# Attention with routing logits: logits from a queue with a rate per group, keys made in two parts, score goes kept whole

## The chip, the core and the metric

The program runs on one core of a Trainium2 chip. The time is the device time of one execution in microseconds, taken as the median of several runs. TensorE multiplies matrices into PSUM, VectorE and ScalarE read and write PSUM and SBUF, GpSimd and SyncE mainly issue transfers here. In the profile the engines are named PE, PEld (TensorE's weight loads), DVE (VectorE), ACT (ScalarE), POOL (GpSimd) and SP (SyncE).

## What is computed

Eight batches of 2496 rows go through an attention with squared ReLU scores; every row of the result is then sent to one of 8 experts, in the order of the logits, each expert taking at most 2496 rows.

```
scores = z @ z.T / 2496                  # per batch, 2496 x 2496, z has 64 columns
x = u * (maximum(scores, 0)**2 @ v)      # 2496 x 256 per batch
logits = x @ w_gate                      # 19968 x 8
order = argsort(-logits.flatten())       # greedy: a row goes to the first expert with room
out[rows of e] = maximum(x[rows of e] @ w1[e], 0) @ w2[e]
```

## The kernel before

The first part, `attention`, takes some 1440 us of the 2565 us span, and the change touches only it. The rows of a batch form 20 key tiles of 128 (the last one of 64 rows, `NT` = 19, `KT` = 20) and five groups of query columns (`NQ` = 5): groups 0 to 3 of 512 columns, group 4 of 448. `seq` lists all 8 x 5 x 20 steps (batch, group, key tile).

For each key tile the scores of a group are three matmuls (`sc`, line 802), since every f32 number is split into a high and a low part. The contraction has 64 rows, so two tiles are multiplied side by side. Ten tiles are done together, in a *go* (`scores`, 30 matmuls): their results leave PSUM through ReLU and scale into `a`, four tiles by VectorE (line 806) and six by ScalarE (line 808). A go is written four steps ahead of the first tile that it serves, so the first go of a group stands before the last four tiles of the group ahead of it. ScalarE then squares each `a` (line 816) and copies it to `hi` (line 820), and VectorE makes `lo` = a - hi (line 829; for the 64-row tile it writes into the same buffer, line 826). `av` multiplies hi and lo with the split values `vh`, `vl` and adds them up in two PSUM tiles, `acc0` and `acc1` (lines 852 to 855; in group 4 with the operands exchanged, lines 844 to 847). There is one buffer of each. At the end of a group VectorE multiplies them with `u` into `xs` (line 865) or, in group 4, `xt` (line 874), and the next group's first matmul into `acc0` may start only when that has read `acc0`. In this document that place is called a *turn*: the turn of group 2 is the passage from group 2 to group 3, and the batch turn that from group 4 to the next batch's group 0.

The logits of a finished group are 32 VectorE instructions (`post_logits`, line 908, tile `lt`): 4 blocks of 128 rows for 8 experts, each a product with a row of weights, added up along the row. They are spread over the steps of the next group. When all logits of a batch are there, `settle` picks each row's best expert and makes sortable keys from its logit (lines 73 to 91 and 104 to 105), at the start of group 2 of the next batch. During each group some z tiles (`zl`, line 772), and in group 4 the 20 value tiles of the next batch (`vl`, line 779), are split on VectorE as well.

All this is written into a table by step, `todo`, and walked in the order of steps. A list scheduler then sets the order of each engine's instructions by readiness in its own model of time; a pin, as in `scores`, keeps squares and splits behind the copies of a go. On the chip every engine then runs its instructions in that fixed order.

Of the kernel before, what the change touches and what calls it, by code (L numbers as in the profile page):

```python
# [21 lines left out]
def tile_attention_then_moe(ctx, tc, u, ut, v, z, w_gate, w1, w2, out):  # L22
# [40 lines left out]
    nc.vector.tensor_scalar(first["at0"], at0_f, 4096.0, -32768.0, op0=OP.mult, op1=OP.add)  # L63

    attention(tc, u, ut, v, z, w_gate, xd, identf, made, first, 1.0 / S)
    moe(tc, xd, first, jp, identf, w1, w2, out, B, S, consts)


def best_expert(nc, pool, first, c, eq):
    lg, m, code, oh = [first[n][:, c] for n in ("lg", "m", "code", "oh")]  # L70
    shape = list(lg.shape)
    cb = first["code8b"][:, None, :].to_broadcast(shape)
    nc.vector.tensor_reduce(m, lg, axis=AX.X, op=OP.max)
    nc.vector.tensor_tensor(eq, lg, m[:, :, None].to_broadcast(shape), op=OP.is_ge)
    nc.vector.tensor_mul(eq, eq, cb)
    nc.vector.tensor_max(eq[:, :, :4], eq[:, :, :4], eq[:, :, 4:])
    nc.vector.tensor_max(eq[:, :, :2], eq[:, :, :2], eq[:, :, 2:4])
    nc.vector.tensor_max(code, eq[:, :, 0], eq[:, :, 1])
    nc.vector.tensor_tensor(oh, code[:, :, None].to_broadcast(shape), cb, op=OP.is_equal)


def order_keys(nc, first, c):
    m, sign, key, rep, top, low = [first[n][:, c] for n in ("m", "sign", "key", "rep", "top", "low")]
    m = m.bitcast(I32)
    nc.vector.tensor_scalar(sign, m, 31, 0x7FFFFFFF, op0=OP.arith_shift_right, op1=OP.bitwise_and)
    nc.vector.scalar_tensor_tensor(key, m, 0x8000, sign, op0=OP.bitwise_xor, op1=OP.bitwise_xor)
    half = key.bitcast(I16).rearrange("p (j h) -> p j h", h=2)
    n = half.shape[1]
    spread(nc, rep, half[:, :, 1])
    nc.vector.tensor_scalar(top, half[:, :, 1], 65536.0, None, op0=OP.mult)  # L90
    nc.vector.tensor_copy(low, half[:, :, 0])
# [9 lines left out]
def spread(nc, rep, x):  # L101
    n = x.shape[1]
    h = n // 2
    nc.scalar.activation(rep[:, :h], x[:, :h, None].to_broadcast([128, h, 8]), AF.Copy)
    nc.vector.tensor_copy(rep[:, h:], x[:, h:, None].to_broadcast([128, n - h, 8]))
# [586 lines left out]
def attention(tc, u, ut, v, z, w_gate, xd, identf, made, first, scale):  # L692
    nc = tc.nc
# [3 lines left out]
    E = lg.shape[2]  # L697
    NT = S // 128
    TL = S - NT * 128
    KT = NT + 1  # L700
    DH = D // 128
    NQ = KT // 4
# [5 lines left out]
    with ExitStack() as ctx:  # L708
# [39 lines left out]
        def load_z(b, g):  # L748
            t = io.tile([128, 512], F32, name="zin")
            for c in range(2):  # L750
                nc.sync.dma_start(t[c * DQ:(c + 1) * DQ], z[b, :, g * 512:(g + 1) * 512])
            ZI[b, g] = t
# [31 lines left out]
        def width(g):  # L784
            return min(512, S - 512 * g)
# [4 lines left out]
        def scores(n, tiles):  # L790
            end = n + tiles
            for n in range(n, end, 2):
                b, g, kt = seq[n]
                w = width(g)
                q = slice(g * 512, g * 512 + w)
                zh, zl = ZH[b], ZL[b]
                p = [ps.tile([128, 512], F32, name="sc", bufs=6)[:, :w] for _ in range(2)]
                for i, (x, y) in enumerate(((zh, zh), (zh, zl), (zl, zh))):
                    for c in range(2):
                        r = slice(c * DQ, (c + 1) * DQ)  # L800
                        k = slice((kt + c) * 128, (kt + c + 1) * 128)
                        nc.tensor.matmul(p[c], x[r, k], y[r, q], start=(i == 0), stop=(i == 2))  # L802
                for c in range(2):
                    a = wk.tile([128, 512], F32, name="a", bufs=GO + 2)[:, :w]
                    if c and n + 2 < end:
                        i = nc.vector.tensor_scalar(a, p[c], 0.0, scale, op0=OP.max, op1=OP.mult)  # L806
                    else:
                        i = nc.scalar.activation(a, p[c], AF.Relu, scale=scale)  # L808
                    A[n + c] = a
                    last[i.ins.engine] = i.ins  # L810
            go.close()
            for i in last.values():
                go.enter_context(tc.issue_after(i))
# [106 lines left out]
            r = slice(TL, 128) if b % 2 else slice(0, TL)  # L920
            nc.vector.tensor_copy(lg[r, B * NT + b // 2], p[r, n * E:(n + 1) * E])

        def settle(lo, hi):
            if lo == hi:
                return
            eq = wk.tile([128, max(NT, B), E], BF, name="eq", bufs=1)
            best_expert(nc, wk, first, slice(lo, hi), eq[:, :hi - lo])
            order_keys(nc, first, slice(lo, hi))

        def premask(lo, hi):  # L930
            at_least(nc, first["mask0"], first["rep"], first["at0"], lo, hi)

        todo = {}
        N = len(seq)

        def at(n, f, *a):
            todo.setdefault(n, []).append((f, a))
# [1 line left out]
        for c in range(0, (B - 1) * NT // 16 * 16, 16):  # L939
            at((B * NQ - 1) * KT + 2 + c // 16, premask, c, c + 16)  # L940
        for b in range(B - 1):
            at(((b + 1) * NQ + 2) * KT, settle, b * NT, (b + 1) * NT)
        at(B * NQ * KT, settle, (B - 1) * NT, (B - 1) * NT + 4 * (NQ - 1))
        at(B * NQ * KT, premask, (B - 1) * NT // 16 * 16, JP - 16)
        for b in range(B):
            for g in range(NQ):
                n0 = (b * NQ + g) * KT
                m0 = n0 + KT
                for d in range(2):
                    at(m0 - 1 if d == 0 else m0 - .5, post_mul if g < NQ - 1 else tail_mul, b, *((g, d) if g < NQ - 1 else (d,)))  # L950
                    if g == NQ - 1:
                        at(m0 + 1 + d if m0 < N else N + 2, tail_turn, b, d)
                t0 = 1 if g < NQ - 1 else 2
                for t in range(4 * E if m0 < N else 0):
                    at(m0 + t0 + t * (KT - 1 - t0) // (4 * E), post_logits, b, g, t // E, t % E)
                if b or g:
                    at(n0 - 3, load_u, b, g)
            n0 = b * NQ * KT
            if b == B - 1:
                at(N + 1, last_logits, b, NQ - 1)  # L960
                at(B * NQ * KT + 3, settle, b * NT + 4 * (NQ - 1), (b + 1) * NT)
                at(B * NQ * KT + 3, settle, B * NT, J)
            if b:
                for g in range(NQ):
                    m = n0 - 3 * KT + 4 * g
                    at(m - 4, load_z, b, g)
                    at(m, z_split, b, g)
                    at(n0 - KT + 4 * g - 8, load_v, b, g)
                for kt in range(KT):
                    at(n0 - KT + kt, split_v, b, kt)  # L970
            else:
                for kt in range(KT):
                    at(kt - 4, split_v, 0, kt)
                for g in range(1, NQ):
                    at((-LA, -2, 2, 4)[g - 1], z_split, 0, g)
                    if g >= 3:
                        at(2 * g - 7, load_z, 0, g)
                        at(4 * g - 11, load_v, 0, g)

        load_z(0, 0)  # L980
        load_v(0, 0)
# [10 lines left out]
        for n in range(-LA, N + 4 * E):  # L992
            if n == 2:
                early.close()
            for k in sorted(k for k in todo if k < n):
                for f, a in todo.pop(k):
                    f(*a)
            if n + LA in goes:
                scores(n + LA, goes[n + LA])
            if 0 <= n + 4 < N:  # L1000
                square(n + 4)
            if 0 <= n + 3 < N:
                split_lo(n + 3)
            if 0 <= n + 4 < N:
                split_hi(n + 4)
            if 0 <= n < N and n % 2 == 0:
                av(n)
            for f, a in todo.pop(n, []):
                f(*a)
# [36 lines left out]
```

## Time and profile before

| | |
|---|---|
| median of 3 runs | 2567.59 us (2567.3 to 2568.21) |
| profiled execution | 2566.36 us, its span 2564.6 us |
| PE busy in the span | 2476.9 us (97%), 19465 matmuls |
| DVE busy | 2035.4 us (79%), 6057 instructions |
| ACT busy | 1526.3 us (60%), 2882 instructions |
| chain that ended last, by engine | PE 85%, DVE 10%, ACT 2% |

Busy time of an engine is the union of its instructions' times; for PE the ends are modelled. The chain that ended last follows the work back from the last instruction to whatever released each step. A row of the timeline gives start and duration in us, engine, line, operation, tiles and shapes, how many equal instructions in a row it stands for, and, in brackets, the idle time ahead of it with what ended it. Instructions of one engine overlap a little in their recorded times, so the step from one start to the next tells how long one holds the engine.

### The profile page before, as it was taken

Reading aid. Unit: us, or ns where it says so; the run is one execution under the profiler, and the core shown is the slowest. Engines: PE = TensorE matmul, PEld = TensorE weight load, DVE = VectorE, ACT = ScalarE, POOL = GpSimd, SP = SyncE. Lnnn points to the kernel's source line nnn. Section 1 sums busy time; section 2 is a strip of 40 time slices with the busy share of each in tenths; the row PEclk is TensorE's granted clock in tenths of the full one; section 3 lists DMA queues with packets and bytes.
Section 4 is the critical chain, followed back from the end, with each engine's and each line's share of the span. In section 5 each row is a group of like instructions: output and inputs, shape, how many; then the busy total and the mean of one; then the engine's idle time right before and its main releaser. Section 6 shows DMA issues by size and latency. Waiting matters only on the chain.

```text
span 2564.6 us, 51297 instructions
## 1 busy us (share of the span) xinstructions
PE 2476.9 (97%) x19465; PEld 2269.6 (88%) x19465; DVE 2035.4 (79%) x6057; ACT 1526.3 (60%) x2882; POOL 359.7 (14%) x507
## 2 busy tenths in 40 slices
PE   8999999999999999999999669999999999999998
PEld 7989989989999999899899557898988898989997
DVE  7898898898898989989988777969695959595322
ACT  8888888797887888878887312333232323233332
POOL 2000000000000000000000003333333333234331
PEclk9999999999999999999999869999999999999999
DMA  5111120121111111111110011211121212131110
GB/s 157 45 59 42 54 74 21 50 74 41 48 58 48 55 58 54 50 41 41 49 33 10 16 42 49 75 49 66 40 72 41 70 42 71 40 99 50 49 40 24
DMA packets 49191, 134.39 MB, mean 52 GB/s; under 512 B 9520, under 2 KB 13104, under 8 KB 48944
## 3 DMA queue, kind: packets, MB, share of 16 engines
q1 hardware_dynamic: 33840, 90.20, 10.9%
q0 software_dynamic: 15104, 40.91, 5.0%
q8 instruction: 152, 2.49, 0.4%
q14 instruction: 95, 0.78, 0.1%
HBM read 90.19 MB, written 40.89 MB: 51 GB/s over the span
## 4 chain that ended last, share of the span: by engine, by line
PE 85%; DVE 10%; ACT 2%; issue 1%; DMA 1%; POOL 0%; POOLq 0%; SPq 0%; ACTq 0%; DVEq 0%
PE acc L852 11%; PE acc L855 11%; PE acc L854 10%; PE sc L802 10%; PE hp L557 5%; PE y L588 5%; PE y L590 5%; PE y L589 5%; PE hp L558 5%; PE hp L559 5%; PE acc L844 2%; PE acc L847 2%; PE acc L846 2%; PE srch L241 2%; DVE lt L908 1%
## 5 line engine op out<-in xcount | busy, mean ns | idle before, releaser
L852 PE MATMUL acc<-vh,hi 128*128 128x256 f32 x2560 | 727.8, 287 | 8.6 <-DVE xs L865 4.7
L855 PE MATMUL acc<-vl,hi 128*128 128x256 f32 x2560 | 718.3, 283 | 0.0
L854 PE MATMUL acc<-vh,lo 128*128 128x256 f32 x2432 | 688.6, 283 | 0.0
L852 PEld LDWEIGHTS acc<-vh,hi 128*128 128x128 f32 x2560 | 489.8, 192 | 37.2 <-issue 22.6
L576 ACT ACTIVATE hh<-hp 128x512 fp32r<-128x512 f32 (+1 forms) x320 | 187.6, 587 | 550.0 <-PE hp L559 460.2
L829 DVE TENSOR_TENSOR lo<-a,hi 128x512 fp32r<-128x512 f32 (+1 forms) x760 | 501.1, 674 | 14.8 <-ACT hi L820 12.6
L855 PEld LDWEIGHTS acc<-vl,hi 128*128 128x128 f32 x2560 | 490.6, 192 | 0.0
L820 ACT ACTIVATE hi<-a 128x512 fp32r<-128x512 f32 (+1 forms) x800 | 470.5, 615 | 29.6 <-ACT a L816 18.9
L908 DVE SCALAR_TENSOR_TENSOR lt<-xs,wgb 128x256 bf16<-128x256 f32 x1248 | 469.5, 421 | 1.6
L854 PEld LDWEIGHTS acc<-vh,lo 128*128 128x128 f32 x2432 | 466.2, 192 | 0.7 <-issue 0.7
L816 ACT ACTIVATE a<-a 128x512 f32<-128x512 f32 (+1 forms) x800 | 463.0, 614 | 0.0
L808 ACT ACTIVATE a<-sc 128x512 f32<-128x512 f32 (+1 forms) x481 | 273.6, 587 | 217.0 <-PE sc L802 191.8
L588 PE MATMUL y<-w2h,hh 128*128 128x256 f32 (+1 forms) x1280 | 365.6, 286 | 0.0
L589 PE MATMUL y<-w2l,hh 128*128 128x256 f32 (+1 forms) x1280 | 361.9, 283 | 0.0
L806 DVE TENSOR_SCALAR a<-sc 128x512 f32<-128x512 f32 (+1 forms) x319 | 210.6, 677 | 138.1 <-PE sc L802 138.0
L557 PE MATMUL hp<-xh,w1h 128*128 128x512 f32 (+2 forms) x646 | 262.6, 408 | 0.7 <-ACT xh L550 0.7
L558 PE MATMUL hp<-xl,w1h 128*128 128x512 f32 (+2 forms) x646 | 251.0, 389 | 0.0
L559 PE MATMUL hp<-xh,w1l 128*128 128x512 f32 (+2 forms) x646 | 249.9, 387 | 0.0
L588 PEld LDWEIGHTS y<-w2h,hh 128*128 128x128 f32 (+1 forms) x1280 | 240.4, 188 | 10.2
L589 PEld LDWEIGHTS y<-w2l,hh 128*128 128x128 f32 (+1 forms) x1280 | 240.2, 188 | 9.0
L621 POOL DMA_INDIRECT out_dram<-y,idx x160 | 179.5, 1122 | 383.7 <-ACT y L615 335.8
L482 POOL DMA_INDIRECT xg<-xd,idx x160 | 161.6, 1010 | 386.7 <-PE xp L541 134.5
(1150 smaller groups left out, 4057.5 us busy)
## 6 DMA issues: line engine op xcount, KB each, us to landing
vr<-in_v_dram SPq DMA_DIRECT2D x32, 512.0 KB, 3.6
ur<-in_u_dram SPq DMA_DIRECT2D x32, 512.0 KB, 4.2
xd<-xs SPq DMA_DIRECT2D x32, 512.0 KB, 2.9
wr<-in_moe_w_dram SPq DMA_DIRECT2D x32, 512.0 KB, 5.0
zin<-in_z_dram SPq DMA_DIRECT2D x80, 128.0 KB, 2.7
ut<-in_ut_dram SPq DMA_DIRECT2D x8, 448.0 KB, 3.8
vr<-in_v_dram SPq DMA_DIRECT2D x8, 384.0 KB, 3.3
xd<-xs SPq DMA_DIRECT2D x8, 384.0 KB, 2.3
```

Source lines behind the costliest of these rows:

```text
L557: nc.tensor.matmul(p[:, c], wh, xh, start=(d == 0), stop=False)
L558: nc.tensor.matmul(p[:, c], wh, xl, start=False, stop=False)
L559: nc.tensor.matmul(p[:, c], wl, xh, start=False, stop=(d == DH - 1))
L588: nc.tensor.matmul(o, h[:, c], wh, start=first, stop=False, skip_group_check=True)
L589: nc.tensor.matmul(o, h[:, c], wl, start=False, stop=False, skip_group_check=True)
L816: nc.scalar.activation(A[n], A[n], AF.Square)
L820: nc.scalar.activation(h, A[n], AF.Copy)
L829: nc.vector.tensor_sub(l, a, h.bitcast(F32))
L852: nc.tensor.matmul(o, h[:, c], vh, start=first and a == 0, stop=False, skip_group_check=True)
L854: nc.tensor.matmul(o, l[:, c], vh, start=False, stop=False, skip_group_check=True)
L855: nc.tensor.matmul(o, h[:, c], vl, start=False, stop=last, skip_group_check=True)
L908: nc.vector.scalar_tensor_tensor(t[r], XS[b, g][r, i], 1.0, WG["rows"][r, e], op0=OP.mult, op1=OP.mult, accum_out=lg[r, j, e:e + 1])
```

## The change

1. A batch's logits go through one queue. A group's 32 logits enter it one step after the group ends (three after group 4), and a step in group g takes RATE[g]/20 of them out: 37, 31, 38, 38 and 18 per group instead of 32. In the last group of the last batch the rate is that of group 0.
2. `settle` for batches 0 to 6 is cut in two, `choose` (best expert) and `rank_keys`, and moved from the start of group 2 of the next batch to steps 12 and 14 of its group 1.
3. The first matmul of the last pair of a go is pinned behind the matmul written before it.

```
-                        nc.tensor.matmul(p[c], x[r, k], y[r, q], start=(i == 0), stop=(i == 2))
+                        mm = nc.tensor.matmul(p[c], x[r, k], y[r, q], start=(i == 0), stop=(i == 2))
+                        if n + tiles == end and i == c == 0:
+                            tc.keep_in_program_order(mm)
...
-        def settle(lo, hi):
-            if lo == hi:
-                return
+        def choose(lo, hi):
             eq = wk.tile([128, max(NT, B), E], BF, name="eq", bufs=1)
             best_expert(nc, wk, first, slice(lo, hi), eq[:, :hi - lo])
+
+        def rank_keys(lo, hi):
             order_keys(nc, first, slice(lo, hi))
+
+        def settle(lo, hi):
+            if lo < hi:
+                choose(lo, hi)
+                rank_keys(lo, hi)
...
         for b in range(B - 1):
-            at(((b + 1) * NQ + 2) * KT, settle, b * NT, (b + 1) * NT)
+            for i, part in enumerate((choose, rank_keys)):
+                at(((b + 1) * NQ + 1) * KT + 12 + 2 * i, part, b * NT, (b + 1) * NT)
...
-                t0 = 1 if g < NQ - 1 else 2
-                for t in range(4 * E if m0 < N else 0):
-                    at(m0 + t0 + t * (KT - 1 - t0) // (4 * E), post_logits, b, g, t // E, t % E)
+                if m0 < N:
+                    ready[m0 + 1 if g < NQ - 1 else m0 + 3] = b, g
...
+        RATE = (37, 31, 38, 38, 18)
+        assert NQ == len(RATE)
+        queue, credit = [], 0.0
+        for n in range(N):
+            if n in ready:
+                queue += [(*ready[n], i, e) for i in range(4) for e in range(E)]
+            g = n // KT % NQ
+            credit += RATE[g if n < N - KT else 0] / KT
+            while queue and credit >= 1:
+                credit -= 1
+                at(n, post_logits, *queue.pop(0))
+            credit = min(credit, 1)
+        assert not queue
```

What this does to the engines' order is shown at three places. In the new file a line of `attention` after the first edit has a number two higher (a logit is L910, `xs` L867).

VectorE in batch 1 at the turn of group 0, from the four copies of the go to the second product; before:

```order
L806 TENSOR_SCALAR a<-sc 128x512 x4
L826 TENSOR_TENSOR hi<-a,hi 64x512
L908 SCALAR_TENSOR_TENSOR lt,lg<-xs,wgb 64x256 x5
L829 TENSOR_TENSOR lo<-a,hi 128x512 x2
L865 TENSOR_TENSOR xs<-acc_2894,ur 128x512
L829 TENSOR_TENSOR lo<-a,hi 128x512
L865 TENSOR_TENSOR xs<-acc_2895,ur 128x512
```

The same place on VectorE now:

```order
L808 TENSOR_SCALAR a<-sc 128x512 x4
L828 TENSOR_TENSOR hi<-a,hi 64x512
L910 SCALAR_TENSOR_TENSOR lt,lg<-xs,wgb 128x256 x8
L831 TENSOR_TENSOR lo<-a,hi 128x512 x2
L910 SCALAR_TENSOR_TENSOR lt,lg<-xs,wgb 128x256
L910 SCALAR_TENSOR_TENSOR lt,lg<-xs,wgb 64x256
L867 TENSOR_TENSOR xs<-acc_2866,ur 128x512
L831 TENSOR_TENSOR lo<-a,hi 128x512
L867 TENSOR_TENSOR xs<-acc_2867,ur 128x512
```

Ten logits stand ahead of the first product where five stood. At the turn of group 1 the order now is the same (8 logits, 2 lo, 2 logits, product); there, before, 5 logits, 11 instructions of `settle` and 2 lo stood ahead of it.

VectorE at the batch turn from batch 0 to 1, from the copies of the go to the first `xt`; before:

```order
L806 TENSOR_SCALAR a<-sc 128x512 x4
L826 TENSOR_TENSOR hi<-a,hi 64x448
L908 SCALAR_TENSOR_TENSOR lt,lg<-xs,wgb 128x256 x5
L779 TENSOR_TENSOR vl<-vr,vh 128x256
L829 TENSOR_TENSOR lo<-a,hi 128x512
L779 TENSOR_TENSOR vl<-vr,vh 128x256
L874 TENSOR_TENSOR xt<-acc_2398,ut 128x448
```

The same place on VectorE now:

```order
L808 TENSOR_SCALAR a<-sc 128x512 x4
L828 TENSOR_TENSOR hi<-a,hi 64x448
L910 SCALAR_TENSOR_TENSOR lt,lg<-xs,wgb 128x256 x6
L779 TENSOR_TENSOR vl<-vr,vh 128x256
L910 SCALAR_TENSOR_TENSOR lt,lg<-xs,wgb 128x256
L831 TENSOR_TENSOR lo<-a,hi 128x512
L779 TENSOR_TENSOR vl<-vr,vh 128x256
L910 SCALAR_TENSOR_TENSOR lt,lg<-xs,wgb 128x256
L831 TENSOR_TENSOR lo<-a,hi 128x512
L876 TENSOR_TENSOR xt<-acc_2398,ut 128x448
```

Three more logits and one more lo stand ahead of `xt`. In the second half of group 4, ahead of these copies, 9 logits now stand where 18 stood.

TensorE in batch 1 at the turn of group 2, from the last matmuls of the old group to the first of the new one (`acc_4532`, now `acc_4524`); before:

```order
L852 MATMUL acc_3968<-vh,hi 128x256
L855 MATMUL acc_3968<-vl,hi 128x256
L802 MATMUL sc<-zh 128x512 x2
L802 MATMUL sc<-zl,zh 128x512 x2
L852 MATMUL acc_4532<-vh,hi 128x256
L854 MATMUL acc_4532<-vh,lo 128x256
```

The same place on TensorE now:

```order
L854 MATMUL acc_3962<-vh,hi 128x256
L857 MATMUL acc_3962<-vl,hi 128x256
L854 MATMUL acc_4524<-vh,hi 128x256
L856 MATMUL acc_4524<-vh,lo 128x256
L857 MATMUL acc_4524<-vl,hi 128x256
```

The four score matmuls that stood in the turn are back in their go, which has 30 again instead of 26. There VectorE has 7 logits, a zl, a lo, 2 logits and 2 lo ahead of the product, where it had 5 logits, a zl and 3 lo. In the same way the one score matmul in each turn of group 3 is gone.

## Rows read from the trace of the kernel before

**Rows 1.** Busy time of each engine in the first 1440 us.

```profile
core 0: us, PE busy (x) PEld busy (x) DVE busy (x) ACT busy (x) POOL busy (x), PEclk, DMA share, GB/s
0.00:1440.00 1440.00, 1419.91 (x10949) 1314.07 (x10950) 1273.28 (x4038) 1183.22 (x2308) 17.05 (x186) 1.00 0.16 52
```

**Rows 2.** Waits of PE until 1420 us: us in total, times, longest.

```profile
PE sc L802 <- DVE a L806: 5.5, 7, 0.8
...
PE acc L852 <- DVE xs L865: 4.7, 7, 0.7
```

**Rows 3.** Timeline of DVE, batch 1, turn of group 1.

```profile
258.75 2.74 DVE L806 TENSOR_SCALAR a<-sc 128x512 f32<-128x512 f32 x4 [3.11 <-PE sc L802]
...
262.24 0.42 DVE L908 SCALAR_TENSOR_TENSOR lt<-xs,wgb 128x256 bf16<-128x256 f32 x1
...
263.98 0.30 DVE L73 TENSOR_REDUCE m<-lg 128x19 f32<-128x152 f32 x1
...
266.71 0.68 DVE L865 TENSOR_TENSOR xs<-acc,ur 128x512 f32<-128x512 f32 x1
```

**Rows 4.** Timeline of PE, same turn: the go's first matmul, the new group's first.

```profile
257.72 0.50 PE L802 MATMUL sc<-zh 64*128 64x512 f32 x2
...
267.54 0.36 PE L852 MATMUL acc<-vh,hi 128*128 128x256 f32 x1 [0.67 <-DVE xs L865]
```

**Rows 5.** Timeline of DVE, batch 1, turn of group 0.

```profile
222.83 2.74 DVE L806 TENSOR_SCALAR a<-sc 128x512 f32<-128x512 f32 x4 [2.89 <-PE sc L802]
...
226.32 0.42 DVE L908 SCALAR_TENSOR_TENSOR lt<-xs,wgb 64x256 bf16<-64x256 f32 x1
...
229.79 0.69 DVE L865 TENSOR_TENSOR xs<-acc,ur 128x512 f32<-128x512 f32 x1 [0.29 <-PE acc L855]
```

**Rows 6.** Timeline of PE, same turn: the old group's last matmul, the new group's first.

```profile
230.67 0.28 PE L855 MATMUL acc<-vl,hi 128*128 128x256 f32 x1
230.79 0.28 PE L852 MATMUL acc<-vh,hi 128*128 128x256 f32 x1
```

**Rows 7.** Timeline of DVE, batch 1, turn of group 2.

```profile
299.05 0.43 DVE L908 SCALAR_TENSOR_TENSOR lt<-xs,wgb 128x256 bf16<-128x256 f32 x1
...
300.79 0.69 DVE L772 TENSOR_TENSOR zl<-zin,zh 128x512 fp32r<-128x512 f32 x1
...
302.49 1.29 DVE L829 TENSOR_TENSOR lo<-a,hi 128x512 fp32r<-128x512 f32 x2 [0.41 <-ACT hi L820]
303.70 1.28 DVE L865 TENSOR_TENSOR xs<-acc,ur 128x512 f32<-128x512 f32 x2
```

**Rows 8.** Timeline of PE, same turn.

```profile
304.53 0.36 PE L852 MATMUL acc<-vh,hi 128*128 128x256 f32 x1 [0.18 <-ACT hi L820]
```

**Rows 9.** Timeline of PE, batch turn from batch 0 to 1.

```profile
184.37 0.51 PE L802 MATMUL sc<-zh 64*128 64x512 f32 x2
...
187.74 0.49 PE L802 MATMUL sc<-zh 64*128 64x512 f32 x1 [0.78 <-DVE a L806]
...
193.94 0.35 PE L852 MATMUL acc<-vh,hi 128*128 128x256 f32 x1
```

**Rows 10.** Timeline of DVE, same turn.

```profile
186.99 2.48 DVE L806 TENSOR_SCALAR a<-sc 128x512 f32<-128x512 f32 x4
189.51 0.62 DVE L826 TENSOR_TENSOR hi<-a,hi 64x448 fp32r<-64x448 f32 x1
190.16 0.43 DVE L908 SCALAR_TENSOR_TENSOR lt<-xs,wgb 128x256 bf16<-128x256 f32 x1
...
191.90 0.42 DVE L779 TENSOR_TENSOR vl<-vr,vh 128x256 fp32r<-128x256 f32 x1
192.23 0.68 DVE L829 TENSOR_TENSOR lo<-a,hi 128x512 fp32r<-128x512 f32 x1
...
193.17 0.62 DVE L874 TENSOR_TENSOR xt<-acc,ut 128x448 f32<-128x448 f32 x1
```

**Rows 11.** Timeline of DVE, batch 1, turn of group 3.

```profile
338.69 0.62 DVE L829 TENSOR_TENSOR lo<-a,hi 128x448 fp32r<-128x448 f32 x1 [0.57 <-ACT hi L820]
```

More of the change, by code (lines that the diff above doesn't have):

```diff
@@ L921, in last_logits @@
             nc.vector.tensor_copy(lg[r, B * NT + b // 2], p[r, n * E:(n + 1) * E])
-        def settle(lo, hi):
-            if lo == hi:
-                return
+        def choose(lo, hi):
             eq = wk.tile([128, max(NT, B), E], BF, name="eq", bufs=1)
             best_expert(nc, wk, first, slice(lo, hi), eq[:, :hi - lo])
+        def rank_keys(lo, hi):
             order_keys(nc, first, slice(lo, hi))
+        def settle(lo, hi):
+            if lo < hi:
+                choose(lo, hi)
+                rank_keys(lo, hi)
         def premask(lo, hi):
             at_least(nc, first["mask0"], first["rep"], first["at0"], lo, hi)
-        todo = {}
+        todo, ready = {}, {}
         N = len(seq)
```

## The prediction

> **What bounds the kernel now.** I read the busy times by stretch first. In the 1440 us of the attention TensorE is busy for 1419.91, VectorE for 1273.28 [rows 1]: TensorE sets the end, and all waits of this part together are 20.09 us, the most that any order could give back here. The reader is to see that VectorE at 88% has room on the average, so that only its order at single places counts. The clock was granted in full (1.00, the 2.4 GHz level) throughout [rows 1]. Then I read whom TensorE waits for [rows 2]: seven times a go waits for VectorE's copies (5.5 us in total), seven times a new group waits for the product that frees its PSUM tile (4.7 us). Seven each, 0.8 and 0.7 us at most: one per batch. The timelines show both.
>
> Turn of group 1, with `settle`. I count t from the first of the go's four copies, 258.75. The logits begin at t = 3.49 (262.24); five take until 263.98, so 0.348 each; then the keys and two lo, and the product starts only at 266.71, t = 7.96 [rows 3]. It ends at 267.39 and the new group's first matmul starts at 267.54 [rows 3, 4]: 0.15 from product to matmul.
>
> Turn of group 0, the same without `settle`. Here the product waited for TensorE (0.29 idle) [rows 5], and the matmuls follow each other every 0.12: 230.67, then the new group at 230.79, t = 7.96, with no wait [rows 6]. So a new group is due at t = 7.96, and the product must start by 7.96 - 0.15 - 0.69 = 7.12. That is my yardstick: a product that starts later than 7.12 costs the difference. Check: with `settle` it started at 7.96, so 0.84 late, and the matmul came at 8.79, which is 0.83 late.
>
> Batch turn. The go starts at 184.37, and copies can begin 1.03 later (257.72 to 258.75 [rows 3, 4]), at 185.40. They begin at 186.99 [rows 9, 10]: the logits and vl of group 4 made VectorE 1.59 late, and TensorE stood still for 0.78 inside the go [rows 9].
>
> **The change part by part.** No instruction is added or removed on VectorE; the 32 logits of a group only move. So the work is to recount, at each of the five turns of a batch, what stands ahead of the product. A lo takes 0.605 (two from 302.49 to 303.70 [rows 7]), a zl as long, a vl 0.33 (191.90 to 192.23 [rows 10]). ScalarE's order hardly changes, and its hi for these lo are there (a lo waits for them 0.41 at the turn of group 2 before, until 302.49 [rows 7]; every lo below that it concerns starts after that).
>
> Turn of group 0, 7 times. Now 8 logits, 2 lo, 2 logits: 3.49 + 2.78 + 1.21 + 0.70 = 8.18, so 1.06 late where nothing was lost: +1.06 each. The 0.29 of idle time that covered it is used up in this.
>
> Turn of group 1, 7 times. `settle` is gone from it, but the order is that of group 0: 8.18 again, 1.06 late instead of 0.83: +0.23. Where the stall goes, the logits are late next. `settle` itself, 1.5 us (263.98 to 266.71 less two lo), now stands in the second half of group 1, where VectorE stood idle for 3.11 before the next copies [rows 3]. That idle time hides it, so I take 0; if a part of it held up a lo that TensorE is about to use, it would cost that part, 0.6 at most (no more than four of its small instructions stand between two lo).
> A rule of the Trainium skill bears on this edit (Perfetto Trace Analysis, section Optimizing Scalar/DVE Operations): where VectorE is not saturated but causes bubbles on another engine, breaking up its instructions may let work complete sooner. By that rule this turn would give its 0.83 back instead of costing 0.23 more, and the sum below would be 14.4 instead of 21.8. The turn of group 0 before agrees with the rule, for with five logits and no `settle` it lost nothing [rows 5, 6]; with ten logits in the place the rows say 8.18, and I go by them.
>
> Turn of group 2, batches 1 to 6. Now 7 logits, a zl, a lo, 2 logits, 2 lo: 3.49 + 2.44 + 0.605 + 0.605 + 0.70 + 1.21 = 9.05, or 1.93 late. Before, the first of the copies was at 299.05 - 3.49 = 295.56 and the new group began at 304.53, t = 8.97 [rows 7, 8], 1.01 late; but in that time TensorE did four score matmuls of the next go, which now are in the go again. Their worth is not shown apart: at most 0.83 (1.01 less the 0.18 idle of [rows 8]), at least 0; I take 4 x 0.12 = 0.48, the step of [rows 6], the nearest row. So the loss goes from 0.53 to 1.93: +1.40 each (1.05 to 1.75 by the bounds). The pin alone thus costs: what filled a wait no longer does.
>
> Turn of group 3. One logit more, 0.348, but the third lo waited 0.57 for ScalarE's hi [rows 11]: covered, 0. The single score matmul there ran without its partner; its removal I take as 0, within -0.2 and +0.1.
>
> Batch turn, 7 times. In the second half of group 4 nine logits fewer (3.1 us) stand on VectorE, more than the 1.59 that it was late: so the copies are on time, at 185.40, and the 0.78 is gained. But then: four copies 2.74, 0.03 to the next, the 64-row lo 0.65 (189.51 to 190.16 [rows 10]); from 188.82 six logits (2.09), then vl, logit, lo, vl, logit, lo (2.57): `xt` starts at 193.48; before, late copies and all, at 193.17 [rows 10]. TensorE began the new group at 193.94, 0.15 behind the end of `xt` [rows 9, 10], and will again: +0.31 net. So the gain is given back some 8 us later, with 0.31 on top (0 if the logits there hide in waits for ScalarE, as at group 3; 1.04, three logits, if the copies come no earlier than before).
>
> Single turns. Batch 0, group 1: 8 logits and 2 lo, 7.48, +0.36; group 2: the fill is lost, +0.48. Batch 7, group 2 (no zl there): as group 0, +1.06; group 3, one logit more among the masks: +0.35. The swap of two loads on SyncE concerns a `u` tile that is used a group later: 0. The tail after the last group has as many logits as before: 0.
>
> Sum: 7 x (1.06 + 0.23 + 0.31) = 11.2; 6 x 1.40 = 8.4; 2.25 for the single turns: +21.8 us. The profiled execution's 2566.36 would become 2588.2; the median before is 1.2 above that execution, so I forecast **2589 us**, slower by 0.85%. Its bounds: 31 turns lose time in this count. If each has 0.3 more room (the idle time of [rows 5], once more), that takes 9.3 off, 12.5 are left, and 9 if the four score matmuls were worth nothing: 2577. If each loses 0.3 more, 31 are reached: 2599.
>
> **The rivals.** The waits go and none comes (faster). The product of a turn is not held by the logits, because they are done before the go (the queue would have to run dry ahead of it). Then 7 x (0.78 + 0.83) at the batch turns and group 1 and 7 x 0.53 at group 2 are saved, 15.0 us: 2553. For it: [rows 2] show just these waits, and VectorE's average has room. Against it: the order on VectorE lists the logits ahead of the product, and the first product of [rows 3] started when the instructions ahead of it were done, not when its input was. It decides up to six logits (3.49 + 2.09 + 1.21 = 6.79); the seventh makes the product late. Chance 6%.
>
> Given back (no difference). TensorE's late start at the turns of groups 0, 1 and 2 is made up in the next go. A go that waited for its copies would allow it; but only the seven batch-turn goes did [rows 2], and the others ran at the matmuls' pace. If it holds, 7 x 0.31 and the 0.35 of batch 7 are left, 2.5: 2570. Chance 6%.
>
> The clock falls (still slower). Four waits of 1 to 1.9 us in a batch, instead of two below 1. If after the six longest 30 matmuls ran at the 1.2 GHz level, their 30 x 0.12 would double: 6 x 3.6 = 22 more, 2611. Against it: granted 1.00 across waits of 0.78 and 0.67 [rows 1, 4, 9]. Chance 3%. The Trainium skill (TensorE: Matmul & The Clock Gate, section A second HAM failure mode: psum-queue depth-cycling) tells of frequent short idles between groups of matmuls that make the clock swing; no run here shows it.
>
> **How the numbers follow.** Forecast 85%, the rivals 6, 6 and 3. The forecast's own bounds, 2577 to 2599, hold most of its 85%, so they are the range. A measurement tells 0.2%, 5 us, from no change: slower than that are the forecast and the clock, 88%; the same 6%; faster 6%.
>
> **What would show it.** In the profile after: waits of `acc` for `xs` at the turns of groups 0 and 1 (some 1.0 us late) and 2 (1.9), and of `acc` for `xt` at the batch turn, where [rows 9] have none; no wait inside the batch-turn go; a product that starts at t = 8.2 behind ten logits; all goes with 30 matmuls. It is wrong if the products start near t = 7 again, or if TensorE's idle time up to 1440 us is not about 20 us more than before.

## The result and the profile after

| | before | after |
|---|---|---|
| median | 2567.71 us (2567.30 to 2568.21) | 2589.99 us (2589.54 to 2590.46) |
| span of the profiled execution | 2564.6 | 2588.2 |
| last matmul of the attention starts at | 1440.61 | 1462.85 |
| first copy of the go at the batch turn 0 to 1, and 6 to 7 | 186.99, 1260.22 (178.87 a batch) | 185.78, 1278.08 (182.05 a batch) |

The changed kernel is slower by 0.88%: ratio 1.0088, 95% interval 1.0076 to 1.0100. Of the 23.6 us that the span grew, 22.2 are in the attention: 3.2 in each batch, counted from one batch turn to the next.

The first view is the busy time of the same 1440 us as [rows 1], now of the changed kernel.

```profile
0.00:1440.00 1440.00, 1393.72 (x10826) 1292.91 (x10827) 1260.39 (x3955) 1171.06 (x2280) 17.03 (x186) 1.00 0.16 52
```

TensorE stands still for 46.28 us instead of 20.09, VectorE is no busier, and the granted clock is 1.00 as before. So the time went into waits. Whom TensorE waits for until 1420 us (us in total, times, longest), as [rows 2]:

```profile
PE acc L854 <- DVE xs L867: 13.9, 10, 1.7
PE acc L854 <- DVE xt L876: 10.1, 7, 1.4
PE acc L854 <- ACT zh L771: 5.3, 6, 0.9
PE acc L854 <- ACT a L818: 5.2, 6, 0.9
```

The seven waits of a go for VectorE's copies are gone. These four rows are 29 waits of a new group for its PSUM tile, all at turns. The two rows that name ScalarE belong to the same waits: at the turn of group 1 the row of TensorE says zh, but VectorE's timeline shows that the product had just ended. VectorE in batch 1 at the turn of group 1, the place of [rows 3] (start, duration, engine, line, operation, idle time ahead in brackets; the short rows that read the sums are left out):

```profile
260.54 0.69 DVE L808 TENSOR_SCALAR a<-sc 128x512 f32<-128x512 f32 x1 [2.67 <-PE sc L802]
...
268.01 0.42 DVE L910 SCALAR_TENSOR_TENSOR lt<-xs,wgb 128x256 bf16<-128x256 f32 x1
...
268.35 0.42 DVE L910 SCALAR_TENSOR_TENSOR lt<-xs,wgb 128x256 bf16<-128x256 f32 x1
...
268.70 0.69 DVE L867 TENSOR_TENSOR xs<-acc,ur 128x512 f32<-128x512 f32 x1
```

TensorE there, as [rows 4]:

```profile
268.38 0.28 PE L857 MATMUL acc<-vl,hi 128*128 128x256 f32 x1
269.53 0.36 PE L854 MATMUL acc<-vh,hi 128*128 128x256 f32 x1 [0.88 <-ACT zh L771]
```

The product starts at t = 268.70 - 260.54 = 8.16 and ends at 269.39, and 0.14 later the matmul comes, t = 8.99. Where a wait has several inputs, the name in the bracket can be wrong; what ended 0.14 earlier is the better guide.

The turn of group 2 on VectorE, the place of [rows 7]:

```profile
297.55 2.74 DVE L808 TENSOR_SCALAR a<-sc 128x512 f32<-128x512 f32 x4 [1.67 <-PE sc L802]
...
303.47 0.69 DVE L772 TENSOR_TENSOR zl<-zin,zh 128x512 fp32r<-128x512 f32 x1
304.07 0.69 DVE L831 TENSOR_TENSOR lo<-a,hi 128x512 fp32r<-128x512 f32 x1
304.68 0.42 DVE L910 SCALAR_TENSOR_TENSOR lt<-xs,wgb 128x256 bf16<-128x256 f32 x1
305.02 0.42 DVE L910 SCALAR_TENSOR_TENSOR lt<-xs,wgb 128x256 bf16<-128x256 f32 x1
305.37 1.29 DVE L831 TENSOR_TENSOR lo<-a,hi 128x512 fp32r<-128x512 f32 x2
306.57 1.28 DVE L867 TENSOR_TENSOR xs<-acc,ur 128x512 f32<-128x512 f32 x2
```

The product starts at t = 9.02. TensorE, as [rows 8]: the new group starts at t = 9.85, after the longest wait of the batch.

```profile
307.40 0.36 PE L854 MATMUL acc<-vh,hi 128*128 128x256 f32 x1 [1.73 <-DVE xs L867]
```

The batch turn from 0 to 1, TensorE as [rows 9]: the go's first matmul, and the new group's.

```profile
184.75 0.50 PE L802 MATMUL sc<-zh 64*128 64x512 f32 x2
...
194.64 0.35 PE L854 MATMUL acc<-vh,hi 128*128 128x256 f32 x1 [1.42 <-DVE xt L876]
```

VectorE there, as [rows 10]:

```profile
185.78 2.75 DVE L808 TENSOR_SCALAR a<-sc 128x512 f32<-128x512 f32 x4
...
193.27 0.68 DVE L831 TENSOR_TENSOR lo<-a,hi 128x512 fp32r<-128x512 f32 x1
193.87 0.61 DVE L876 TENSOR_TENSOR xt<-acc,ut 128x448 f32<-128x448 f32 x1
```

The copies are on time (1.03 after the go's first matmul), the wait inside the go is gone, and the new group begins 9.89 after the go's first matmul instead of 9.57: given back, with 0.32 on top.

### The profile page after: what moved, and what is told of

Read it like the earlier page. It is cut to its first block, busy times and chain, and to the rows that moved or that the text cites. A ratio compares the mean times of both kernels' runs of the same rounds, so it can differ in the third digit from the quotient of the medians.

```text
span 2588.2 us, 51283 instructions
## 1 busy us (share of the span) xinstructions
PE 2474.4 (96%) x19465; PEld 2269.3 (88%) x19465; DVE 2043.3 (79%) x6057; ACT 1528.3 (59%) x2882; POOL 362.5 (14%) x507
## 4 chain that ended last, share of the span: by engine, by line
PE 79%; DVE 12%; ACT 4%; issue 2%; DMA 1%; POOL 0%; POOLq 0%; SPq 0%; DVEq 0%; ACTq 0%
PE acc L854 10%; PE sc L802 10%; PE acc L857 9%; PE acc L856 9%; PE hp L557 5%; PE y L588 5%; PE y L590 5%; PE y L589 5%; PE hp L558 5%; PE hp L559 5%; PE acc L846 2%; PE acc L849 2%; PE acc L848 2%; DVE lt L910 2%; ACT a L818 2%
## 5 line engine op out<-in xcount | busy, mean ns | idle before, releaser
L910 DVE SCALAR_TENSOR_TENSOR lt<-xs,wgb 128x256 bf16<-128x256 f32 x1248 | 467.7, 420 | 1.7
L588 PEld LDWEIGHTS y<-w2h,hh 128*128 128x128 f32 (+1 forms) x1280 | 240.3, 188 | 10.2
```

The source lines that it names most:

```text
L588: nc.tensor.matmul(o, h[:, c], wh, start=first, stop=False, skip_group_check=True)
L910: nc.vector.scalar_tensor_tensor(t[r], XS[b, g][r, i], 1.0, WG["rows"][r, e], op0=OP.mult, op1=OP.mult, accum_out=lg[r, j, e:e + 1])
```

## The experiments

Eight kernels ran, in two sets of four. The second set ran on another chip, where the part after the attention took some 47 us longer (the kernel before: median 2614.21 instead of 2566.83 in the first set). So kernels are compared by their ratio to the kernel before on the same chip, and by the time at which the last matmul of the attention starts (in us). The only trace of the kernel before is from the first chip; the attention itself keeps the same pace on both, since from one undisturbed turn to the next copies start 35.92 us apart in before (turns of groups 0 and 1 of batch 0) as in keep19z (batch 1). The second set is queue_only, r34, keep19z and keep19z_nopin. t is that of the first product in batch 1.

| kernel | ratio, 95% interval | end of attention | t of g0, g1, g2 |
|---|---|---|---|
| before | | 1440.61 | 6.96, 7.96, 8.14 |
| after | 1.0088 (1.0076 to 1.0100) | 1462.85 | 8.16, 8.16, 9.02 |
| pin_only | 1.0015 (1.0006 to 1.0024) | 1444.49 | 6.96, 7.97, 8.14 |
| no_pin | 1.0082 (1.0068 to 1.0095) | 1461.32 | 8.16, 8.16, 9.02 |
| settle_only | 0.9974 (0.9964 to 0.9984) | 1433.82 | 6.96, 6.96, 8.15 |
| keep | 0.9964 (0.9951 to 0.9978) | 1430.44 | 6.96, 6.96, 8.14 |
| queue_only | 1.0075 (1.0052 to 1.0098) | 1461.53 | 8.16, 8.00, 9.03 |
| r34 | 1.0024 (1.0009 to 1.0038) | 1444.47 | 7.82, 7.13, 8.14 |
| keep19z | 0.9916 (0.9899 to 0.9934) | 1420.38 | 6.96, 6.96, 6.96 |
| keep19z_nopin | 0.9932 (0.9914 to 0.9951) | 1421.16 | 6.96, 6.96, 6.96 |

**Edit 3 alone, and all without it.**

> The kernel before with edit 3 alone (goes kept whole). Theory: the pin costs only the fill of the turn of group 2, where four score matmuls stood in a wait: 7 times 0.48, so 3.4 us more than before, 2571 (0 to 5.8 more by the bounds of the prediction). Rival, the pin is the cause: most of the 22 us that the whole change costs appear here, 2585 or more. In the profile the theory expects a wait of some 1.0 us at the turn of group 2 and nothing new elsewhere.

One correction to point 3 of the change: the condition `n + tiles == end` holds for a go's first pair, since the loop starts at `n = end - tiles`. So the matmul that is pinned is the first of the whole go, and the four score matmuls that stood in the turn of group 2 were the first four of their go.

Measured: 2570.53 us, the attention 3.9 us longer, and 0.46 a batch from one batch turn to the next (1.4 in batch 0, of which 0.9 stand before its first turn). The waits of TensorE until 1420 us, in that kernel:

```profile
PE acc L854 <- ACT hi L822: 8.5, 8, 2.5
...
PE sc L802 <- DVE a L808: 5.6, 7, 0.8
PE acc L854 <- DVE xs L867: 4.8, 7, 0.7
```

The two groups of [rows 2] stand as they were. The first row has grown: it is one wait of 2.5 at the start, which the kernel before has too, and seven at the turn of group 2, where 0.18 [rows 8] became 0.86; it is named by the lo's input (the products of [rows 7] and here both start at t = 8.14). The fill is thus worth 0.46 a batch, two pairs of score matmuls at the 0.23 that a pair takes inside a go.

> The changed kernel without edit 3. Theory: VectorE's order at the turns is what it was with the pin, so all waits stay but that of group 2, which has its four score matmuls again: 7 times 0.48 less than the changed kernel, 2586.6. Rival, the pin is the cause: the time goes back to 2568 to 2570.

Measured: 2587.25 us, the attention 1.5 us shorter than after; the longest wait for `xs` fell from 1.7 to 1.1, seven of 0.2 at the turn of group 3 went, and the other waits stayed. The pin is a small part of the loss in both directions.

**Edit 2 alone.** The kernel before with

```
...
-            at(((b + 1) * NQ + 2) * KT, settle, b * NT, (b + 1) * NT)
+            for i, part in enumerate((choose, rank_keys)):
+                at(((b + 1) * NQ + 1) * KT + 12 + 2 * i, part, b * NT, (b + 1) * NT)
```

> The kernel before with edit 2 alone: settle cut in two and moved into the second half of group 1, logits as before. Theory: the product of the turn of group 1 stands behind five logits and two lo, t = 3.49 + 1.74 + 1.21 = 6.44, before the 7.12 at which it is due, so the 0.83 of that turn is gone 7 times and nothing comes in its place: 5.8 us less than before, 2562. Rival, the time is given back by a lo that the two parts hold up, or by the next go: 2566 to 2568.

Measured: 2559.95 us, the attention 6.8 us shorter, 0.90 a batch. At the turn of group 1 VectorE now stands idle ahead of the product and TensorE's matmul releases it:

```profile
265.20 0.69 DVE L865 TENSOR_TENSOR xs<-acc,ur 128x512 f32<-128x512 f32 x1 [0.29 <-PE acc L855]
```

So edit 2 does gain, and nothing takes the settle's place as long as five logits stand there. The rule that was weighed in the prediction (the Trainium skill, Perfetto Trace Analysis, section Optimizing Scalar/DVE Operations: instructions broken up may let work complete sooner) is not tested by this run nor by the whole change: the instructions of `settle` were not broken up, they moved whole, in two parts. What gained is the freed place ahead of the product.

**Edit 1 alone.** The changed kernel without the pin and with `settle` at its old step.

> Edit 1 alone: the changed kernel without the pin and with settle back at the start of group 2. Theory (the product waits for whatever stands ahead of it): at the turn of group 1 eight logits and three instructions of settle stand ahead of the product, t = 3.49 + 2.78 + 1.21 + some 0.6 = 8.1, as late as the ten logits without it (8.17); the rest of settle slides behind the product. So settle costs nothing here, and edit 1 alone costs nearly the whole: 2586 to 2588, as the changed kernel without the pin (2587.25). Rival, the edits add up: edit 2 took 6.9 us off the kernel before, so it would be missing here: 2594.

Measured: ratio 1.0075, which is 2587 on the 2567.7 of before; the attention 20.9 us longer, as without the pin (20.7). The gains do not add up: behind ten logits it is all the same whether `settle` is there. Seven logits stay, `m`, `eq` and `sign` of `settle` and one logit more make t = 8.00.

**The logits kept behind the product.** In the changed kernel a logit must come after the product written last:

```
...
+            done["x"] = nc.vector.tensor_mul(XS[b, g][:, c], acc, UR[b, g][:, c]).ins
...
+            with tc.issue_after(done["x"]):
                 nc.vector.scalar_tensor_tensor(t[r], XS[b, g][r, i], 1.0, WG["rows"][r, e], ...
```

> The changed kernel with one more ordering: a logit may not go ahead of the product written before it (issue_after of the latest xs or xt). Queue, rates, settle and pin stay. Now 6, 5 and 6 logits stand ahead of the products of groups 0, 1 and 2 instead of 10, 10 and 9, and 3 instead of 8 ahead of xt. Theory (logits ahead of the product are the cause): the products of groups 0 and 1 start by t = 3.49 + 2.09 + 1.21 = 6.79, no wait; group 2 at 3.49 + 2.09 + 0.6 + 1.8 = 7.98, 0.86 late instead of 1.90; the batch turn has no wait at all. Two logits now stand between the two products of a turn, which makes the second some 0.3 late at groups 0 and 1. Against before, per batch: -0.83 -0.78 +0.33 +0.6 = -0.7, so 5 us less, 2563 (2556 to 2568). Rival, the turn waits come from something that the queue does elsewhere (VectorE too full, buffers of lt, transfers): the time stays at 2580 or more.

Measured: 2557.2 us; from 22.2 us more than before to 10.2 less in the attention. Queue, rates, settle and pin are those of the change: the order of logits and products alone made the difference. VectorE in batch 1 at the turn of group 0, first copy and product (t = 6.96):

```profile
222.36 2.74 DVE L808 TENSOR_SCALAR a<-sc 128x512 f32<-128x512 f32 x4 [3.11 <-PE sc L802]
...
229.32 0.69 DVE L867 TENSOR_TENSOR xs<-acc,ur 128x512 f32<-128x512 f32 x1
```

The run also shows where the ten logits of that turn came from: with this edge six are left, so four were written behind the product, two at the last step of the group (they now stand between the two products) and two at steps of the next group. They were ready, because the queue still held logits of an older group: counted from RATE, 9, 10 and 4 are left in it when groups 0, 1 and 2 end. That the list scheduler moved them ahead is shown by the edge that stops it; that it did so because the product in its model still waited for TensorE is argued. In the kernel before nothing is left at that point: the next logits need the product itself.

The theory had the sign and the places right and the size some 5 us too small. The two logits between the products cost 0.06 instead of 0.3, and the batch turn gained 1.1 instead of 0.78. At the turn of group 2 the product still starts at t = 8.14, and TensorE's seven waits of 0.86 are there as in pin_only. The count of VectorE's instructions gave 7.98; t is 8.14 behind five logits (before, pin_only) and behind six (here, r34), so one logit more costs nothing there: in [rows 7] the lo wait 0.41 for ScalarE's hi, and the logit stands in that wait.

**A dose.** The changed kernel with `RATE = (34, 34, 34, 34, 34)`.

> The changed kernel with the rate 34 in every group instead of 37, 31, 38, 38 and 18; settle and pin as changed. A dose within one kernel: nine logits stand ahead of the product of group 0, seven at group 1, six (with a zl and three lo) at group 2, none of the queue's at group 3 beyond six. Theory (0.348 for each logit beyond six): group 0 starts its product at t = 7.83, 0.71 late; group 1 at 7.14, 0.02 late, so no wait to speak of; group 2 at 3.49 + 2.09 + 0.6 + 1.82 = 8.0, 0.9 late. The go of the batch turn waits again, by 0.8 to 1.4, since group 4 has some 34 logits again. Per batch against before: 0.71 - 0.81 + 0.37 + (0 to 0.6) = 0.3 to 0.9; 2569 to 2574. Rival (the number of logits ahead is not what counts, the queue is): waits at all three turns as in the changed kernel, 2585 or more.

Measured: ratio 1.0024, which is 2574; the attention 3.9 us longer. TensorE at the turns of groups 0 and 1 in batch 1, the new group's first matmul:

```profile
231.13 0.36 PE L854 MATMUL acc<-vh,hi 128*128 128x256 f32 x1 [0.53 <-DVE xs L867]
...
267.11 0.36 PE L854 MATMUL acc<-vh,hi 128*128 128x256 f32 x1
```

VectorE's first copy and the product at the same two turns:

```profile
222.48 2.74 DVE L808 TENSOR_SCALAR a<-sc 128x512 f32<-128x512 f32 x4 [3.11 <-PE sc L802]
...
230.30 0.68 DVE L867 TENSOR_TENSOR xs<-acc,ur 128x512 f32<-128x512 f32 x1
...
259.15 2.74 DVE L808 TENSOR_SCALAR a<-sc 128x512 f32<-128x512 f32 x4 [2.00 <-PE sc L802]
...
266.28 0.68 DVE L867 TENSOR_TENSOR xs<-acc,ur 128x512 f32<-128x512 f32 x1
```

Behind nine logits the product starts at t = 7.82 (expected 7.83) and TensorE waits; behind seven it starts at 7.13 (expected 7.14) and TensorE does not. In one kernel, with one queue, the number of logits ahead decides. And the number is the leftover: counted from RATE, 3, 1 and 0 logits are left in the queue when groups 0, 1 and 2 end, and nine, seven and six stand ahead. In batches 2, 4 and 6 nine stand at the turn of group 0 too, but the product starts at t = 8.31, for a reason that has nothing to do with the queue (Group 0, below). The go of the batch turn waited 0.5 at most, less than the 0.8 to 1.4 that were expected.

**A version almost without waits.** The kernel keep, and

```
...
-                    m = n0 - 3 * KT + 4 * g
+                    m = n0 - 3 * KT + 3 * g
...
-            credit += RATE[g if n < N - KT else 0] / KT
+            if n % KT in (19,) and n < N - KT:
+                continue
+            credit += RATE[g] / (KT - len((19,))) if n < N - KT else RATE[0] / KT
```

> The kernel keep with two more edits: no logit is issued at the last step of a group, so none stands between the two products of a turn (the rate of the other steps is raised by 20/19), and the five zl of a batch stand three steps apart instead of four, so none is in the turn of group 2. Theory: products of groups 0, 1 and 2 at t = 3.49 + 2.09 + 1.21 = 6.79, no wait in any of the five turns; of the 2.14 a batch that the kernel before lost at turns nothing is left: 7 x 2.14 = 15, so 2552 (2550 to 2555), some 6 us less than keep. Rival: the turn of group 2 waits for ScalarE's hi instead of the product, and the 0.86 stays: 2557.

Measured: ratio 0.9916, the attention 20.2 us shorter than before and 42.5 shorter than after; 2546 by the ratio, the fastest kernel here. That is below the 2550 to 2555 that were expected, in the main because the expectation took the loss at the batch turn as 0.78 (see the bound, below). The waits of TensorE until 1400 us that are over 1 us in total:

```profile
PE sc L802 <- ACT zh L771: 4.9, 1, 4.9
PE acc L854 <- ACT hi L822: 2.5, 1, 2.5
PE acc L846 <- DVE xs L867: 1.6, 7, 0.2
```

The two single ones are the start; of the turns only seven of 0.2 are left, at group 3. The turn of group 2 on VectorE in this kernel:

```profile
292.68 2.74 DVE L808 TENSOR_SCALAR a<-sc 128x512 f32<-128x512 f32 x4 [0.72 <-PE sc L802]
...
298.26 1.29 DVE L831 TENSOR_TENSOR lo<-a,hi 128x512 fp32r<-128x512 f32 x2
299.64 0.69 DVE L867 TENSOR_TENSOR xs<-acc,ur 128x512 f32<-128x512 f32 x1
```

The z tile's split is out of this turn, with its zl on VectorE and its zh on ScalarE, and two lo instead of three stand ahead: the product starts at t = 6.96 there too. Which of the three did it was not tried apart.

> The same kernel without the pin (edit 3 undone). One score matmul then stands in the turn of group 3, all other goes have 30. Theory: where no turn waits there is nothing to fill, so the pin is worth nothing: the same time as with it, within 1.5 us. Rival, keeping goes whole has a worth of its own: 2 us or more slower than with the pin.

Measured: ratio 0.9932, and the attention ends 0.8 us later. The medians are 3.5 us apart, but the intervals overlap, so the whole time does not decide between theory and rival. By the end of the attention the pin is worth 0.8 us here, as expected where hardly anything waits.

## Why the prediction was right, point by point

Forecast 2589 us, measured 2589.99. The method, counting t at each turn from what stands ahead of the product, held to a few hundredths but for the turn of group 0 in three batches. The sum (21.8, measured 22.2 in the attention) is nearer than its terms: 0.7 at the turns of group 0 and at least 0.7 in the matmuls of group 4 (last section) were not counted, while 0.4 at the start of the attention and 0.4 at the turns of group 2 came off. That these nearly cancel is luck.

- **Group 0** (t = 8.18): 8.16 in batches 1, 3, 5 and 7; 8.39 in 2, 4 and 6. In those the last logit is one of 64 rows that lie in partitions 64 to 127 (`r = slice(TL, 128)`, an odd batch's logits); in the other four it lies in partitions 0 to 63. Batch 2:

```profile
413.04 0.42 DVE L910 SCALAR_TENSOR_TENSOR lt<-xs,wgb 128x256 bf16<-128x256 f32 x1
...
413.50 0.42 DVE L910 SCALAR_TENSOR_TENSOR lt<-xs,wgb 64x256 bf16<-64x256 f32 x1
...
413.96 0.69 DVE L867 TENSOR_TENSOR xs<-acc,ur 128x512 f32<-128x512 f32 x1
```

  The two steps are 0.46 where 0.35 is usual, with 31 ns of idle time ahead of each: three times 0.23 that were not counted. Every change between those 64 rows and 128 costs this here, and none does with the lower 64: r34 has four such changes at the same turn, and its product comes 0.49 later (8.31 instead of 7.82).
- **Group 1** (8.18): 8.16, and the matmul 0.20 later than in [rows 4] (t = 8.99 instead of 8.79); counted 0.23. That `settle` costs nothing at its new place is shown by settle_only.
- **Group 2** (9.05): 9.02, the matmul at 9.85. The fill, taken as 0.48 between 0 and 0.83, measured 0.46 by pin_only. (The lower bound of that term, 1.05, was worked out wrongly: with a fill worth nothing it is 1.93 - 1.01 = 0.92.)
- **Group 3** (0): t = 7.21 in both kernels; in pin_only the new group starts 0.10 earlier without the score matmul, and the next copies follow 0.11 later behind that.
- **Batch turn** (+0.31): +0.32 from the go's first matmul. Copies and `xt` came 0.38 and 0.39 later than the times forecast, as the go itself began 0.38 later.
- **The bound of 20.09 us was wrong.** The prediction called TensorE's idle time "the most that any order could give back", and the rival that all waits go was put at 15 us. keep19z took 20.2 us out of the attention, while TensorE's idle time until 1400 us fell only from 19.84 to 9.78 (1390.22 of them busy):

```profile
0.00:1400.00 1400.00, 1390.22 (x10838) 1294.95 (x10839) 1264.31 (x3965) 1166.27 (x2282) 16.95 (x186) 1.00 0.17 53
```

  The idle time in a bracket leaves out two things. The ends of matmuls are modelled, and a matmul's recorded length (0.28 at the turn of [rows 6], 0.39 in a go) is longer than the step to the next (0.12, 0.23), so each wait costs some 0.16 more than its bracket says: 0.67 in [rows 4] stands for 0.83. And the matmuls of a go run two at a time; at the batch turn of [rows 9] the wait fell between two of a pair, so that one ran alone ahead of it and one alone at the end of the go:

```profile
186.56 0.39 PE L802 MATMUL sc<-zh 64*128 64x512 f32 x1
```

  The bracket there says 0.78. From this matmul to the next, at 187.74, it is 1.18 instead of 0.23, and from the go's first matmul to the new group's first 9.57. Without any wait, in keep19z from batch 1 to 2, the latter takes 8.27:

```profile
359.99 0.50 PE L802 MATMUL sc<-zh 64*128 64x512 f32 x2
...
368.26 0.30 PE L854 MATMUL acc<-vh,hi 128*128 128x256 f32 x1
```

  So 1.30 were lost there, not 0.78. The forecast did not suffer, as it went by starts and not by idle time; the reach of the rival did.
- **The rivals.** Given back: no; the goes after late turns kept their pace, and all of it stayed. The clock: 1.00 through waits of up to 1.74 us. The Trainium skill's rule on frequent short idles between groups of matmuls (TensorE: Matmul & The Clock Gate, section A second HAM failure mode: psum-queue depth-cycling) is not borne out by this trace, where some thirty such waits left the granted clock at 1.00.

What the prediction did not name is why the logits stood there. It read them off the order; the runs keep and r34 show that it was the leftover in the queue.

## What to carry to other kernels

A queue that still holds ready work lets a list scheduler put it ahead of the one instruction that the next stage needs. Pin such filler behind that instruction, as keep does, or let the queue run empty before it, as in the kernel before. Count what stands ahead of each releasing instruction and compare its start with the time at which it is due: here each logit beyond the room cost its full 0.35 us, and a gain and a loss at the same place did not add up: edit 2 alone took 6.8 us off, and beside edit 1 only 0.2 (20.9 and 20.7 us lost in the attention). Take what a wait costs from start to start against an undisturbed place, not from the idle time beside it.

## What was not expected of the hardware

- In the second half of group 4 the matmuls with 448 columns follow each other every 0.2026 us on the average in batches 1 to 3 of the kernel before and every 0.2067 in those of the kernel after, 59 of them in a row, at a granted clock of 1.00 in both: 0.23 a batch. Both values occur in several of the kernels here (keep19z has either, by batch). Its cause stays open.
- On the chip of the second set the part after the attention took 1170 to 1173 us from the last matmul of the attention to the end of the span, against 1124 to 1126 on the first, in kernels that do not differ there. From keep to keep19z, 49 us in all, TensorE stands still for 35 us more in that part and is busy for 14 more. In keep19z four of its waits, 15.6 us in total, are for ScalarE at line 588, which the kernels of the first chip do not list among their longest. As each of the four ended, after 3.9 us, the granted clock fell to 0.50 (the 1.2 GHz level), three times for 3.4 us and once for 6.9; in keep it is 1.00 from 1544 to 2547 us. Why the waits are there on one chip and not on the other was not pursued.
